# Early gated attention of a fused kernel: scans of four pairs, masks, key copies and products of two, scores in quarters of the array

## The chip, the cores and the metric

The kernel runs on one core of a Trainium2 chip. The metric is the time of one launch on the device in microseconds, and lower is better. TensorE (PE) multiplies matrices, VectorE (DVE), ScalarE (ACT) and GpSimd (POOL) do the elementwise work, and SyncE (SP) issues most of the DMAs. The first section of the kernel uses all of them at once.

## The reference

What is computed is a gated linear attention and, on its output, two expert layers in turn (4 x 768 = 3072 tokens, 8 heads of 48, width 384).

```python
for t in range(S):
    state = alpha[:, :, t, :, None] * state + np.einsum('bhd,bhe->bhde', k[:, :, t], v[:, :, t])
    y[:, :, t] = np.einsum('bhd,bhde->bhe', q[:, :, t], state)
...
h = x @ w_in                       # 384 -> 2048
x = (h * sigmoid(h)) @ w_out       # 2048 -> 384
g = x @ w_gate                     # 384 -> 1536
return (silu(g) * (x @ w_val)) @ w_out2
```

All tensors are float32 in value; the weights come as 64-bit floats and are decoded to 32 bits on the chip.

## The kernel before, in words

The sequence of each batch is cut into chunks of C = 128 tokens: 6 x 4 = 24 chunks, each with 8 heads in NP = 4 pairs. A pair lies on the 128 partitions, head 0 on rows 0 to 47 and head 1 on rows 64 to 111. Per pair the decay from each token to the end of its chunk is a product of alphas, made by a scan that runs backward (`stage_a1`, tile `r`); its counterpart from the start, scaled by the reciprocal of the whole, is made by a second scan (`stage_a3`, tile `g`). Keys are multiplied by `r`, queries by `g` (tile `kq`). Then the scores of a head are one product, a causal mask makes `pt` of them, and the output `y` (in the accumulator `yd`) is `pt` times values plus the queries times the carried state. The state of the next chunk needs the keys transposed (`kt`, made by a product with the identity) times the values.

The first NF = 7 chunks, 28 pairs, are made ahead of everything else; this document calls them the early attention. In it the products run in full float32. A "duo" d is two pairs, so a chunk is duos 2n and 2n + 1. The scans, the reciprocals and the products with keys and with queries are issued per duo, the masks, key copies and score products per pair. The loop `for g in range(first): attn(2)` writes the instructions in the order in which each engine runs them; nothing reorders them afterwards. `filler` puts a bfloat16 product without use ahead of scores, into accumulator columns that are overwritten later. `spread` (GpSimd) lays out the values of pair 0 of the first four chunks once more, so that its rows can be added into the other pairs' spare rows. `chunk_high` and `chunk_end` split the finished output into a high and a low part (`x`), add up the state, and load the values of chunk n + 2 (`load_v`). The input of chunk n + 2 (`load_in`) is loaded into one of two buffers once chunk n's products have been made.

Beside this, `units1` decodes weights of the first expert layer. One unit is 128 x 384 weights: three steps on VectorE (`decode`, L93, L98 and L103), then a high part on ScalarE and a low part on GpSimd or VectorE. In the early attention one call of `units1` follows each chunk from the third on, with the three steps belonging to two neighbouring units.

After the early attention the expert layer begins: `g1(0)` is the hidden product of the first block (tokens of chunks 0 to 3), `act1` its activation in two parts, `gh` (ScalarE) and `gl` (VectorE, L322), and `g2` the second product, which needs `gh` at L770 and L771 and `gl` at L773. The other 17 chunks of attention (the late attention) are made beside the expert layer, with their scores in high and low parts (`qh`, `ql`, `kh`, `kl`).

Of the kernel before, what the change touches and what calls it, by code (L numbers as in the profile page):

```python
# [20 lines left out]
DM = H * D  # L21
# [247 lines left out]
def fast(ctx, tc, pk, w1, w2, out, bad_i):  # L269
# [49 lines left out]
    cp.tile([128, 112], F32, name="edge")  # L319
# [12 lines left out]
    qh = ac.tile([128, NP, 2 * C + 2 * D], F32R, name="qh")  # L332
    ql = ac.tile([128, NP, 2 * C], F32R, name="ql")
    kts = [ac.tile([128, 2, 64], F32, name=f"kt{i}") for i in range(NP + 1)]
# [3 lines left out]
    ones = ac.tile([128, 2, CA], F32, name="ones")  # L338
    rc_t = [ac.tile([128, 2, CA], F32, name=f"rc{i}") for i in range(2)]
# [5 lines left out]
    p0 = [start[:, (7 + 2 * i) * C:(9 + 2 * i) * C].rearrange("p (h t) -> p h t", h=2) for i in range(2)]  # L345
# [52 lines left out]
    def KF(d):  # L398
        return DVE if d == 0 else POOL

    def stage_a1(d):
        n, ps_, _ = duo(d)
        lo = ps_.start * CA
        r = r_t[d] = ap.tile([128, 272], F32, tag="r", name=f"r{d}")[:, :2 * CA].rearrange(
# [5 lines left out]
            data1=ones.rearrange("p i t -> p (i t)")[:, ::-1], initial=0.0,  # L412
# [3 lines left out]
    def stage_a2(d):  # L416
        n, ps_, _ = duo(d)
        kq_t[d] = ap.tile([128, 2, 2, C], F32, tag="kq", name=f"kq{d}", bufs=6)
        DVE.reciprocal(out=rc_t[d % 2][:, :, 0], in_=r_t[d][:, :, 0])  # L419
        KF(d).tensor_tensor(  # L420
            out=kq_t[d][:, 0], in0=in_t[n][1][:, 0, ps_], in1=r_t[d][:, :, 1:], op=ALU.mult
        )

    def stage_a3(d):
        n, ps_, (c, b) = duo(d)
        lo = ps_.start * CA
        gg = ap.tile([128, 272], F32, tag="g", name=f"g{d}")[:, :2 * CA].rearrange(
# [4 lines left out]
            data1=rc_t[d % 2].rearrange("p i t -> p (i t)"), initial=0.0,  # L432
            op0=ALU.mult, op1=ALU.add,
        )
        (DVE if d == 0 else POOL).tensor_tensor(
# [3 lines left out]
        if c and n < NF:  # L439
            for i in range(ps_.start, ps_.stop):  # L440
                s = state[b][:, i]
                ACT.activation(out=s, in_=s, func=AF.Copy, scale=r[:, i - ps_.start, 0:1])
        elif c:
# [10 lines left out]
    def q_parts(d):  # L454
        _, ps_, _ = duo(d)
        for h in range(2):
            r, cs = slice(64 * h, 64 * h + 64), slice(C * h, C * h + C)
            yield qh[r, ps_, cs], ql[r, ps_, cs], kq_t[d][r, 1], h

    def stage_b(d):  # L460
        kh = kh_t[d] = ap.tile([128, 2, C], F32R, tag="kh", name=f"kh{d}")
# [4 lines left out]
    def stage_c(d):  # L466
        kl = kl_t[d] = ap.tile([128, 2, C], F32R, tag="kl", name=f"kl{d}")
# [4 lines left out]
    def guard(d):  # L472
# [3 lines left out]
            out=jk, in_=kq_t[d].rearrange("p x i t -> p (x i t)"), func=AF.Square,  # L476
            accum_out=sums[:, ps_.start // 2, n:n + 1],
# [5 lines left out]
    def qkt(g):  # L483
# [3 lines left out]
        kf, qf = kq_t[d][:, 0, i], kq_t[d][:, 1, i]  # L487
        if n < NF:

            b = pools_ps["early"].tile([128, 2, 512], F32, tag=f"s{g % 2}", name=f"s{g}")  # L490
            for h in range(2):
                r = slice(64 * h, 64 * h + 64)
                PE.matmul(b[:, h, :C], kf[r], qf[r], start=True, stop=True)
            PE.matmul(b[:, 0, C:C + 2 * D], kf, columns(ident), start=True, stop=True)
            s_t[g] = b[:, :, :C], b[:, 0, C:C + 2 * D]
            return
        b = bank(5, f"s{g}")
        w = 2 * C + (2 * D if n < NCH - B else 0)
        kh, kl = kh_t[d][:, i], kl_t[d][:, i]
        PE.matmul(b[:, :w], kh, qh[:, p, :w], start=True, stop=False)  # L500
# [9 lines left out]
    def filler(g):  # L510


        n, i = divmod(g, NP)


        if n and i < 2:
            return
        if n not in y_t:
            yd_place(n)
        wide = mask.rearrange("p (o t) -> p o t", o=1).to_broadcast([128, 4, C])  # L520
        for _ in range(3 if 0 < g < NP + 2 else 1):
# [3 lines left out]

    def causal(g):
        if g < NE * NP and g % NP == 0:
# [1053 lines left out]
```

## Time and profile before

| | before |
|---|---|
| time, median of 3 runs | 936.69 us (935.79 to 937.24) |
| the profiled execution | 938.12 us, of which the span is 936.3 us |
| TensorE | 915.2 us busy, 98% of the span |
| VectorE, ScalarE, GpSimd | 618.1, 453.0, 287.9 us busy |
| granted TensorE clock | 0.992 on average |
| HBM | 118 MB read, 30 MB written |

The span is the time from the first to the last instruction of the profiled execution; its 938.12 us include what lies around it. Busy shares are averages over a program that has stages with different limits, so the rows below are taken from single stages.

### The profile page before, as it was taken

The numbers are of one execution on the slowest core, as the hardware profiler recorded it, in microseconds if no ns is written. First come the engines' busy times: TensorE is split into PE (matmuls) and PEld (weight loads), VectorE is DVE, ScalarE is ACT, GpSimd is POOL, SyncE is SP. The second block draws the span as 40 slices with busy tenths as digits, with TensorE's granted clock in tenths as the row PEclk, the third lists the DMA queues.
The fourth block names the chain that finished last, engine by engine and source line by source line (L and its number), as shares of the span: only waits on it lengthen the run. The fifth ranks groups of instructions, "written<-read, shape, count | busy, mean of one in ns | idle before, by whom it ended". The sixth has DMA issues, their size and how long they took to land.

```text
span 936.3 us, 14380 instructions
## 1 busy us (share of the span) xinstructions
PE 915.2 (98%) x5210; PEld 779.6 (83%) x5210; DVE 618.1 (66%) x1107; ACT 453.0 (48%) x1019; POOL 287.9 (31%) x401
## 2 busy tenths in 40 slices
PE   9989999999999999999999999999999999999996
PEld 5669998889999998988888888878888888888785
DVE  8889936656577668465268366786477875577732
ACT  3545435646465565555346344543544454444432
POOL 5430006528779789686228000000000000000000
PEclk9899999999999999999999999999999999999998
DMA  7854203243645554532375486532757503755302
GB/s 235 300 187 153 85 1 105 80 142 119 194 160 194 167 175 161 181 108 101 118 264 208 157 299 224 185 114 85 244 213 267 194 10 135 269 205 214 121 0 71
DMA packets 43007, 150.89 MB, mean 161 GB/s; under 512 B 4400, under 2 KB 9008, under 8 KB 40240
## 3 DMA queue, kind: packets, MB, share of 16 engines
q1 hardware_dynamic: 42304, 149.30, 46.3%
q8 instruction: 43, 0.70, 0.3%
q10 hardware_dynamic: 624, 0.59, 0.2%
q14 instruction: 36, 0.29, 0.1%
HBM read 118.03 MB, written 29.88 MB: 158 GB/s over the span
## 4 chain that ended last, share of the span: by engine, by line
PE 89%; DVE 5%; issue 2%; DMA 1%; POOL 1%; ACT 1%; SPq 0%; ACTq 0%; POOLq 0%; DVEq 0%
PE o L1158 15%; PE h L721 7%; PE x L773 7%; PE x L770 7%; PE x L771 7%; PE h L722 7%; PE h L724 7%; PE A L1095 5%; PE D L1095 5%; PE E L1095 5%; PE yd L562 2%; PE K L1095 2%; PE F L1095 2%; PE C L1095 2%; PE B L1095 2%; PE G L1095 2%
## 5 line engine op out<-in xcount | busy, mean ns | idle before, releaser
L322 DVE TENSOR_TENSOR gl<-h,gh 128x384 fp32r<-128x384 f32 (+1 forms) x112 | 68.5, 612 | 89.8 <-ACT h L739 84.4
L721 PE MATMUL h<-x,w 128*128 128x384 f32 (+1 forms) x336 | 122.7, 365 | 1.8 <-DMA x<-y 1.8
L770 PE MATMUL x<-gh,w 128*128 128x384 f32 (+1 forms) x336 | 121.5, 362 | 0.4 <-ACT gh L738 0.4
L771 PE MATMUL x<-gh,w 128*128 128x384 f32 (+1 forms) x336 | 121.2, 361 | 0.0
L722 PE MATMUL h<-x,w 128*128 128x384 f32 (+1 forms) x336 | 120.9, 360 | 0.0
L738 ACT ACTIVATE gh<-h 128x384 fp32r<-128x384 f32 (+1 forms) x112 | 59.9, 534 | 105.3 <-PE h L724 103.4
L1158 PE MATMUL o<-gh,ring 128*128 128x512 f32 x288 | 88.8, 389 | 0.0
L773 PE MATMUL x<-gl,w 128*128 128x384 f32 (+1 forms) x336 | 84.5, 359 | 1.6 <-DVE gl L322 1.6
L724 PE MATMUL h<-x,w 128*128 128x384 f32 (+1 forms) x336 | 84.3, 358 | 0.0
L420 POOL TENSOR_TENSOR kq<-in,r 128x256 f32<-128x256 f32 x47 | 43.0, 915 | 130.1 <-DVE rc L419 76.3
L721 PEld LDWEIGHTS h<-x,w 128*128 128x128 f32 x336 | 63.1, 188 | 10.6 <-issue 5.4
L770 PEld LDWEIGHTS x<-gh,w 128*128 128x128 f32 x336 | 63.1, 188 | 6.7 <-ACT gh L738 1.1
L773 PEld LDWEIGHTS x<-gl,w 128*128 128x128 f32 x336 | 61.3, 188 | 8.1 <-DVE gl L322 2.3
L771 PEld LDWEIGHTS x<-gh,w 128*128 128x128 f32 x336 | 63.1, 188 | 5.2
L722 PEld LDWEIGHTS h<-x,w 128*128 128x128 f32 x336 | 63.1, 188 | 5.1
L724 PEld LDWEIGHTS h<-x,w 128*128 128x128 f32 x336 | 61.3, 188 | 5.9
L1158 PEld LDWEIGHTS o<-gh,ring 128*128 128x128 f32 x288 | 54.1, 188 | 11.2
L739 ACT ACTIVATE h<-h 128x384 f32<-128x384 f32 (+1 forms) x112 | 59.5, 532 | 0.0
L322 DVE TENSOR_TENSOR gl<-a,gh 128x512 fp32r<-128x512 f32 x48 | 32.9, 692 | 37.3 <-ACT gh L1147 36.2
L1158 PE MATMUL o<-gl,ring 128*128 128x512 f32 x144 | 56.4, 392 | 0.8 <-DVE gl L322 0.8
L1095 PE MATMUL A<-mov,ring 128*128 128x512 f32 x198 | 55.7, 389 | 0.0
L1095 PE MATMUL D<-mov,ring 128*128 128x512 f32 x198 | 55.6, 389 | 0.0
(211 smaller groups left out, 1983.3 us busy)
## 6 DMA issues: line engine op xcount, KB each, us to landing
ring<-comb_d SPq DMA_DIRECT2D x21, 1920.0 KB, 7.7
raw<-in_w_dram SPq DMA_DIRECT2D x58, 384.0 KB, 4.4
in<-in_pk_dram SPq DMA_DIRECT2D x22, 770.5 KB, 4.4
ring<-wo_d SPq DMA_DIRECT2D x6, 1920.0 KB, 7.3
comb_d<-area SPq DMA_DIRECT2D x8, 896.0 KB, 5.4
in_v<-in_pk_dram SPq DMA_DIRECT2D x24, 256.0 KB, 3.7
comb_d<-area SPq DMA_DIRECT2D x8, 640.0 KB, 4.9
x1r<-x_d SPq DMA_DIRECT2D x6, 768.0 KB, 8.9
```

What stands on the lines that cost most here:

```text
L322: eng.tensor_tensor(out=lo, in0=src, in1=hi.bitcast(F32), op=ALU.subtract)
L420: KF(d).tensor_tensor(out=kq_t[d][:, 0], in0=in_t[n][1][:, 0, ps_], in1=r_t[d][:, :, 1:], op=ALU.mult)
L721: PE.matmul(acc, part(u, k), xh, start=(k == 0), stop=False)
L722: PE.matmul(acc, part(u, k, 1), xh, start=False, stop=False)
L724: PE.matmul(acc, part(u, k), xl, start=False, stop=(k == len(xk) - 1))
L738: ACT.activation(out=gh, in_=hb, func=AF.Silu)
L739: ACT.activation(out=hb, in_=hb, func=AF.Silu)
L770: PE.matmul(x1_t[j][m], part(u, m), gh, start=(f == 0), stop=False)
L771: PE.matmul(x1_t[j][m], part(u, m, 1), gh, start=False, stop=False)
L773: PE.matmul(x1_t[j][m], part(u, m), gl, start=False, stop=(f == NF1 - 1))
L1095: PE.matmul(acc, s(hs, r), x[:, hx], start=op in new and i == 0, stop=i == 2, skip_group_check=True,)
L1158: PE.matmul(o_t[b][m], part(ring_t[p, f], m, l), x, start=(f == 0 and i == 0), stop=(f == NF2 - 1 and i == 2),)
```

## The change

The early attention gets functions of its own, and the loop over pairs becomes a loop over duos (`early`).

- Scans: `scan_r` and `scan_g` run over all four pairs of a chunk (516 elements instead of 258), with one reciprocal of four elements. Chunk 0 alone keeps two halves.
- Products: keys and queries of a duo lie side by side and are multiplied in one instruction of 512 elements (GpSimd; VectorE for the first duo). A duo's tile has 48 more columns that hold parts of the identity, written once at the start into six fixed tiles (`kqs`).
- Scores: a head's product with the queries and its product with the identity become one, whose moving operand is 176 columns wide. It is issued for half of the keys at a time, so that it takes 64 rows and 64 columns of the array: 8 products for a duo (`scores2`).
- Mask and key copy: one instruction for a duo instead of one for a pair (`mask2`, `keys2`).
- Decode: from chunk 3 on `early_unit` runs all three steps of one unit in a row; its temporary lies in columns of the accumulator `yd` of the next chunk, which are not yet in use, and no longer in SBUF.
- The tiles of the late attention (`qh`, `ql` and others) are opened, zeroed (GpSimd) and filled with the identity (ScalarE, four copies) between the early attention and `g1(0)` instead of at the start (`open_late`).
- Fillers: one for each duo, four ahead of the second duo.

On VectorE this stands for one chunk and a little more before (names are tiles: `r`, `g` the scans, `pt` and `start` the masks, `x` the low part of an output, `dec` and `raw` a decode):

```order
L409 SCALAR_TENSOR_TENSOR r_422<-in_332,ones 128x258
L419 RECIPROCAL rc_115<-r_422 128x2
L430 SCALAR_TENSOR_TENSOR g_452<-in_332,rc_115 128x258
L93 TENSOR_SCALAR dec_0_457<-raw_0_189 128x384
L532 TENSOR_TENSOR pt_459<-s_448,mask 128x256
L532 TENSOR_TENSOR pt_471<-s_467,mask 128x256
L409 SCALAR_TENSOR_TENSOR r_475<-in_332,ones 128x258
L419 RECIPROCAL rc_116<-r_475 128x2
L322 TENSOR_TENSOR x_309<-yd_381,x_309 128x3x128
L532 TENSOR_TENSOR pt_490<-s_486,mask 128x256
L430 SCALAR_TENSOR_TENSOR g_493<-in_332,rc_116 128x258
L532 TENSOR_TENSOR pt_506<-s_502,mask 128x256
```

and here for the same part after (`rg` the scans, `rc` the reciprocals, `yd` and `raw` the decode in the accumulator):

```order
L422 SCALAR_TENSOR_TENSOR rg_115<-in_270,ones_113 128x516
L427 RECIPROCAL rc_114<-rg_115 128x4
L474 TENSOR_TENSOR pt_397<-s_368,mask 128x512
L435 SCALAR_TENSOR_TENSOR rg_115<-in_270,rc_114 128x516
L93 TENSOR_SCALAR yd_366<-raw_0_178 128x384
L98 SCALAR_TENSOR_TENSOR yd_366<-raw_0_178,yd_366 128x384
L103 SCALAR_TENSOR_TENSOR raw_0_178<-raw_0_178,yd_366 128x384
L322 TENSOR_TENSOR x_273<-yd_300,x_273 128x3x128
L474 TENSOR_TENSOR pt_431<-s_422,mask 128x512
```

Four scans of 258 have become two of 516, four masks two. The scan of the next chunk's queries, the whole decode and the subtraction now follow each other, and the mask of the chunk's second duo stands behind them.

On TensorE these are, before, the scores of the last three pairs of chunk 3 and the first of chunk 4, behind which the value products of chunk 3 stand (`s` the scores, `yd<-mask` the filler):

```order
L493 MATMUL s_448<-kq_344 128x128 x2
L494 MATMUL s_448<-start,kq_344 128x96
L522 LDWEIGHTS mask
L522 MATMUL yd_465<-mask 128x512
L493 MATMUL s_467<-kq_393 128x128 x2
L494 MATMUL s_467<-start,kq_393 128x96
L522 LDWEIGHTS mask
L522 MATMUL yd_465<-mask 128x512
L493 MATMUL s_486<-kq_393 128x128 x2
L494 MATMUL s_486<-start,kq_393 128x96
L493 MATMUL s_502<-kq_424 128x128 x2
L494 MATMUL s_502<-start,kq_424 128x96
```

and after, with chunk 3's second duo, chunk 4's first, and the first value products of chunk 3:

```order
L609 LDWEIGHTS mask
L609 MATMUL yd_366<-mask 128x512
L463 MATMUL s_422<-kq_118 64x176 x8
L609 LDWEIGHTS mask
L609 MATMUL yd_439<-mask 128x512
L463 MATMUL s_441<-kq_119 64x176 x8
L650 MATMUL yd_366<-pt_397,in_v_343 64x128
```

The scores of a pair were two products of 64 rows and one of 128; a duo's are now eight of 64 rows and 64 columns. The value products of a chunk now follow the scores of the next chunk's first duo instead of its first pair.

On SP's queue, from the load of chunk 2's input on, before (`in` inputs, `in_v` values, `raw` weights):

```order
L365 DMA in_187<-in_pk_dram 128x1541
L689 DMA raw_0_189<-in_w_dram 128x768
L689 DMA raw_1_191<-in_w_dram 128x768
L365 DMA in_253<-in_pk_dram 128x1541
L689 DMA raw_2_298<-in_w_dram 128x768
L389 DMA in_v_318<-in_pk_dram 128x512
L365 DMA in_332<-in_pk_dram 128x1541
L689 DMA raw_3_334<-in_w_dram 128x768
```

and after:

```order
L385 DMA in_190<-in_pk_dram 128x1541
L385 DMA in_211<-in_pk_dram 128x1541
L385 DMA in_270<-in_pk_dram 128x1541
L409 DMA in_v_277<-in_pk_dram 128x512
L787 DMA raw_2_280<-in_w_dram 128x768
L787 DMA raw_3_298<-in_w_dram 128x768
L385 DMA in_337<-in_pk_dram 128x1541
L409 DMA in_v_343<-in_pk_dram 128x512
```

The load of the values of chunk n + 2 stood ahead of the load of the input of chunk n + 4; now it stands behind it.

```diff
-    def KF(d):
-        return DVE if d == 0 else POOL
+    def scan_r(n, i, k):
+        rg, cs = rg4[n % 2], slice(i * CA, (i + k) * CA)
+        DVE.tensor_tensor_scan(
+            out=rg[:, 0, cs][:, ::-1], data0=in_t[n][0][:, cs.start + 1:cs.stop + 1][:, ::-1],
+            data1=ones4[:, i:i + k].rearrange("p i t -> p (i t)")[:, ::-1], initial=0.0,
+            op0=ALU.mult, op1=ALU.add,
+        )
+        DVE.reciprocal(
+            out=rc4[:, i:i + k, 0], in_=rg[:, 0].rearrange("p (i t) -> p i t", i=NP)[:, i:i + k, 0]
+        )
+    def scan_g(n, i, k):
+        rg, cs = rg4[n % 2], slice(i * CA, (i + k) * CA)
+        DVE.tensor_tensor_scan(
+            out=rg[:, 1, cs], data0=in_t[n][0][:, cs],
+            data1=rc4[:, i:i + k].rearrange("p i t -> p (i t)"), initial=0.0, op0=ALU.mult, op1=ALU.add,
+        )
+        by_pair = rg.rearrange("p x (i t) -> p x i t", i=NP)
+        for lo in range(i, i + k, 2):
+            d = (n * NP + lo) // 2
+            kq_t[d] = kqs[d % 6]
+            (DVE if d == 0 else POOL).tensor_tensor(
+                out=kq_t[d][:, :, :2 * C].rearrange("p i (x t) -> p x i t", x=2),
+                in0=in_t[n][1][:, :, lo:lo + 2], in1=by_pair[:, :, lo:lo + 2, 1:], op=ALU.mult,
+            )
+        c, b = divmod(n, B)
+        if c:
+            for p in range(i, i + k):
+                t = state[b][:, p]
+                ACT.activation(out=t, in_=t, func=AF.Copy, scale=by_pair[:, 0, p, 0:1])
+        if i + k == NP:
+            load_in(n + 2)
+    def scores2(d):
+        b = pools_ps["early"].tile([128, 2, 512], F32, tag=f"s{d % 2}", name=f"s{d}")
+        for i in range(2):
+            for h in range(2):
+                r, cs = slice(64 * h, 64 * h + 64), slice(i * (C + D), (i + 1) * (C + D))
+                for t in (slice(0, 64), slice(64, 128)):
+                    PE.matmul(
+                        b[t, h, cs], kq_t[d][r, i, t], kq_t[d][r, i, C:], start=True, stop=True,
+                        skip_group_check=True,
+                    )
+        return b[:, :, :2 * (C + D)].rearrange("p h (i x) -> p i h x", i=2)
+    def mask2(d, s):
+        pt = ap.tile([128, 2, 2, C], F32, tag="pt", name=f"pt{d}", bufs=3)
+        pt_t[2 * d], pt_t[2 * d + 1] = pt[:, 0], pt[:, 1]
+        wide = mask.rearrange("p (a o t) -> p a o t", a=1, o=1).to_broadcast([128, 2, 2, C])
+        DVE.tensor_tensor(out=pt, in0=s[:, :, :, :C], in1=wide, op=ALU.mult)
+    def keys2(d, s):
+        t = kts[d % 3]
+        kt_t[2 * d], kt_t[2 * d + 1] = (t[:, i].rearrange("p h x -> p (h x)") for i in range(2))
+        ACT.activation(out=t[:, :, :, :D], in_=s[:, :, :, C:], func=AF.Copy)
+    def early(d):
+        m, odd = divmod(d, 2)
+        if m not in y_t:
+            yd_place(m)
+        filler(m, 4 if d == 1 else 1)
+        s = scores2(d)
+        if not odd and m:
+            pv(m - 1)
+        mask2(d, s)
+        keys2(d, s)
+        if odd:
+            if m and m + 2 < NF:
+                scan_r(m + 2, 0, NP)
+        elif m + 1 < NF:
+            if m < 2:
+                scan_r(m + 1, 0, NP)
+            scan_g(m + 1, 0, NP)
+        if m < NE and odd == (m == 0):
+            spread(m)
+        if not odd and m:
+            if m >= 3:
+                early_unit(yd_t[m][:, 512:])
+            chunk_high(m - 1)
+            chunk_end(m - 1)
+        up_to("gd", d - 1, guard, ND)
+        up_to("l1", d, load1, NU1)
...
-        kf, qf = kq_t[d][:, 0, i], kq_t[d][:, 1, i]
-        if n < NF:
-            b = pools_ps["early"].tile([128, 2, 512], F32, tag=f"s{g % 2}", name=f"s{g}")
-            for h in range(2):
-                r = slice(64 * h, 64 * h + 64)
-                PE.matmul(b[:, h, :C], kf[r], qf[r], start=True, stop=True)
-            PE.matmul(b[:, 0, C:C + 2 * D], kf, columns(ident), start=True, stop=True)
-            s_t[g] = b[:, :, :C], b[:, 0, C:C + 2 * D]
...
-    def filler(g):
...
+    def filler(n, times):
         wide = mask.rearrange("p (o t) -> p o t", o=1).to_broadcast([128, 4, C])
-        for _ in range(3 if 0 < g < NP + 2 else 1):
+        for _ in range(times):
             PE.matmul(
                 yd_t[n][:, :512].rearrange("p (o t) -> p o t", o=4), mask, wide, start=True, stop=True
             )
...
+    def decode_in(key, bank_):
+        if raw_t[key].dtype != F32:
+            dec_t[key] = bank_.bitcast(I32)[:, :DM]
+            in_bank.add(key)
+        for i in range(3):
+            decode_unit(key, i)
...
+    def early_unit(bank_):
+        u = st["d1"]
+        up_to("s1", st["h1"] - 1, lambda u: low_unit(("1", u), POOL), NU1)
+        up_to("h1", st["f1"] - 1, lambda u: high_unit(("1", u), wp, "w"), NU1)
+        if u < st["l1"]:
+            decode_in(("1", u), bank_)
+            for k in "d1", "e1", "f1":
+                st[k] = u + 1
...
     make_identity(nc, ident)
+    for t in kqs:
+        one, two = (
+            ident[:, c:c + D].rearrange("p (o d) -> p o d", o=1).to_broadcast([128, 2, D]) for c in (0, 64)
+        )
+        POOL.tensor_tensor(out=t[:, :, 2 * C:], in0=one, in1=two, op=ALU.add)
...
-    POOL.memset(qh.bitcast(F32), 0.0)
-    POOL.memset(ql.bitcast(F32), 0.0)
...
     first = NF * NP
-    st["b"] = st["c"] = first // 2
-    stage_a(0)
-    stage_a(1)
     up_to("l1", 1, load1, NU1)
-    for i in range(NP):
-        ACT.activation(
-            out=qh[:, i, 2 * C:].rearrange("p (h d) -> p h d", h=2), in_=columns(ident), func=AF.Copy
-        )
-    T0 = 2
-    for g in range(first):
-        attn(2)
-        if g % 2:
-            up_to("l1", g // 2, load1, NU1)
+    for i in (0, 2):
+        scan_r(0, i, 2)
+        scan_g(0, i, 2)
+    for d in range(first // 2):
+        early(d)
+    st["qk"], st["pv"] = first, NF - 1
+    for k in "a1", "a2", "a3", "b", "c":
+        st[k] = first // 2
...
     need1(1)
     units1()
     attn(1, False)
+    up_to("gd", first_d - 1, guard, ND)
+    estack.close()
+    open_late()
     g1(0)
     rest = act1(*steps[0])
     units1()
```

## Rows read from the trace of the kernel before

**Rows 1.** Stages of the span; busy us (instructions) by engine, granted clock, DMA share.

```profile
0.00:58.10 58.10, 52.41 (x506) 36.26 (x506) 49.26 (x102) 26.35 (x96) 28.18 (x51) 0.91 0.73 255
67.00:120.00 53.00, 52.98 (x275) 48.72 (x274) 52.14 (x115) 26.26 (x56) 0.51 (x1) 1.00 0.38 129
```

**Rows 2.** Groups of instructions in the stage 0 to 58.1 us.

```profile
L430 DVE TENSOR_TENSOR_SCAN g<-in,rc 128x258 f32<-128x258 f32 x14 | 12.2, 869 | 1.0 <-DVE rc L419 0.5
L409 DVE TENSOR_TENSOR_SCAN r<-in,ones 128x258 f32<-128x258 f32 x14 | 11.8, 845 | 2.0 <-DMA in<-in_pk_dram 1.9
L532 DVE TENSOR_TENSOR pt<-s,mask 128x256 f32<-128x256 f32 x24 | 9.6, 412 | 2.6 <-PE s L494 2.6
L419 DVE RECIPROCAL rc<-r 128x2 f32<-128x2 f32 x14 | 2.4, 168 | 0.5
L435 POOL TENSOR_TENSOR kq<-in,g 128x256 f32<-128x256 f32 x13 | 9.3, 718 | 10.3 <-DVE g L430 10.3
L593 POOL COPY start<-in_v 128x96 f32<-128x96 f32 x4 | 1.8, 462 | 0.0
L612 ACT ACTIVATE x<-yd 128x384 fp32r<-128x384 f32 x6 | 2.9, 485 | 0.0
L1350 ACT ACTIVATE qh<-start 128x96 fp32r<-128x96 f32 x4 | 0.8, 270 | 0.6 <-POOL qh L1337 0.6
```

**Rows 3.** Order of time, from the last mask to the first low part.

```profile
55.72 0.41 DVE L532 TENSOR_TENSOR pt<-s,mask 128x256 f32<-128x256 f32 x1
58.13 0.50 PE L721 MATMUL h<-x,w 128*128 128x512 f32 x1
60.57 0.49 ACT L644 ACTIVATE x<-yd 48x384 fp32r<-48x384 f32 x1 [1.93 <-DVE y L322]
66.19 0.97 PE L773 MATMUL x<-gl,w 128*128 128x512 f32 x3 [1.60 <-DVE gl L322]
```

**Rows 4.** Order of time, a scan alone and one beside GpSimd.

```profile
6.12 0.69 DVE L409 TENSOR_TENSOR_SCAN r<-in,ones 128x258 f32<-128x258 f32 x1
6.90 0.68 POOL L420 TENSOR_TENSOR kq<-in,r 128x256 f32<-128x256 f32 x1 [1.37 <-DVE r L409]
7.05 1.08 DVE L430 TENSOR_TENSOR_SCAN g<-in,rc 128x258 f32<-128x258 f32 x1
```

**Rows 5.** Groups of decoding before 55.8 us; one such step through PSUM later.

```profile
L93 DVE TENSOR_SCALAR dec<-raw 128x384 int32<-128x384 int32 x4 | 2.8, 707 | 0.1
L103 DVE SCALAR_TENSOR_TENSOR raw<-raw 128x384 int32<-128x384 int32 x3 | 2.5, 821 | 0.0
L98 DVE SCALAR_TENSOR_TENSOR raw<-raw,dec 128x384 int32<-128x384 int32 x3 | 2.0, 668 | 0.0
...
473.03 0.56 DVE L98 SCALAR_TENSOR_TENSOR dec<-raw,dec 128x384 int32<-128x384 int32 x1
```

**Rows 6.** Order of time on TensorE, score blocks, value and state products.

```profile
24.36 0.49 PE L493 MATMUL s<-kq 64*128 64x128 f32 x4
25.18 0.45 PE L562 MATMUL yd<-pt,in_v 128*64 128x128 f32 x4
27.15 0.38 PE L493 MATMUL s<-kq 64*128 64x128 f32 x2
...
49.51 0.65 PE L583 MATMUL yd<-kq,state 64*48 64x128 f32 x16
```

**Rows 7.** DMA issues of 0 to 60 us: the values of a chunk.

```profile
in_v<-in_pk_dram SPq DMA_DIRECT2D x8, 256.0 KB, 5.7
```

**Rows 8.** Seconds of the stage, columns as in group 1.

```profile
35.00:36.00 1.00, 0.24 (x2) 0.00 (x0) 0.96 (x3) 0.00 (x0) 0.57 (x1) 1.00 1.03 419
37.00:38.00 1.00, 1.00 (x6) 0.78 (x6) 0.97 (x3) 0.68 (x3) 0.33 (x1) 0.50 0.99 386
43.00:44.00 1.00, 1.00 (x16) 0.54 (x8) 1.00 (x2) 0.00 (x0) 0.32 (x1) 0.63 1.01 388
65.00:66.00 1.00, 0.00 (x0) 0.00 (x0) 1.00 (x2) 0.42 (x1) 0.12 (x1) 1.00 0.51 174
```

More of the change, by code (lines that the diff above doesn't have):

```diff
@@ L331, in fast @@
     ac = astack.enter_context(tc.tile_pool(name="ac", bufs=1))
-    qh = ac.tile([128, NP, 2 * C + 2 * D], F32R, name="qh")
-    ql = ac.tile([128, NP, 2 * C], F32R, name="ql")
-    kts = [ac.tile([128, 2, 64], F32, name=f"kt{i}") for i in range(NP + 1)]
+    kts = [ac.tile([128, 2, 2, 64], F32, name=f"kt{i}") for i in range(3)]
     jk = ac.tile([128, 4 * C], BF16, name="jk")
@@ L337, in fast, with open_late @@
     mask = ac.tile([128, C], BF16, name="mask")
-    ones = ac.tile([128, 2, CA], F32, name="ones")
-    rc_t = [ac.tile([128, 2, CA], F32, name=f"rc{i}") for i in range(2)]
+    estack, lstack = ExitStack(), ExitStack()
+    ep = estack.enter_context(tc.tile_pool(name="ep", bufs=1))
+    ones4 = ep.tile([128, NP, CA], F32, name="ones4")
+    rc4 = ep.tile([128, NP, CA], F32, name="rc4")
+    rg4 = [ep.tile([128, 2, NP * CA], F32, name=f"rg{i}") for i in range(2)]
+    kqs = [ep.tile([128, 2, 2 * C + D], F32, name=f"kq{i}") for i in range(6)]
+    late_t = {}
+    def open_late():
+        lp = late_t["pool"] = lstack.enter_context(tc.tile_pool(name="lp", bufs=2))
+        for name, w, dtype in (("qh", 2 * C + 2 * D, F32R), ("ql", 2 * C, F32R)):
+            late_t[name] = lp.tile([128, NP, w], dtype, tag=name, name=name, bufs=1)
+            POOL.memset(late_t[name].bitcast(F32), 0.0)
+        for i in range(NP):
+            ACT.activation(
+                out=late_t["qh"][:, i, 2 * C:].rearrange("p (h d) -> p h d", h=2), in_=columns(ident),
+                func=AF.Copy,
+            )
+        for name in ("ones", "rc0", "rc1"):
+            t = late_t[name] = lp.tile([128, 2, CA], F32, tag=name, name=name, bufs=1)
+            POOL.memset(t, 0.0)
+        POOL.memset(late_t["ones"][:, :, C:], 1.0)
     start = big(0, "start")
@@ L411, in stage_a1 @@
             data0=in_t[n][0][:, lo + 1:lo + 2 * CA + 1][:, ::-1],
[L412 removed]
+            data1=late_t["ones"].rearrange("p i t -> p (i t)")[:, ::-1], initial=0.0,
             op0=ALU.mult, op1=ALU.add,
@@ L438, in stage_a3 @@
         r = r_t.pop(d)
[L439 to L443, printed above, removed]
+        if c:
             POOL.tensor_tensor(
@@ L475, in guard @@
         ACT.activation(
-            out=jk, in_=kq_t[d].rearrange("p x i t -> p (x i t)"), func=AF.Square,
-            accum_out=sums[:, ps_.start // 2, n:n + 1],
+            out=jk.rearrange("p (x t) -> p x t", x=2),
+            in_=kq_t[d][:, :, :2 * C] if n < NF else kq_t[d].rearrange("p x i t -> p x (i t)"),
+            func=AF.Square, accum_out=sums[:, ps_.start // 2, n:n + 1],
         )
@@ L584, in pv @@
                     y[r:r + D, p * C:p * C + C], state[b][hs, p],
-                    kq_t[(first + p) // 2][hs, 1, p % 2], start=False, stop=True,
+                    kq_t[(first + p) // 2][(hs, p % 2, slice(C, 2 * C)) if n < NF else (hs, 1, p % 2)],
+                    start=False, stop=True,
                     skip_group_check=True,
@@ L695, in decode_unit @@
                 dec_t[key] = mp.tile([128, DM], I32, tag="dec", name="dec%s_%d" % key, bufs=1)
-            x = decode(DVE, raw_t[key], dec_t[key], step, inplace=key[0] == "2" and key[1] >= NW)
+            x = decode(DVE, raw_t[key], dec_t[key], step, inplace=key in in_bank)
             if step == 2:
@@ L956, in units_o @@
         if f < NF2:
-            if raw_t["2", NW + f].dtype != F32:
-                dec_t["2", NW + f] = bank(5, f"dec{f}").bitcast(I32)[:, :DM]
-            for i in range(3):
-                decode_unit(("2", NW + f), i)
+            decode_in(("2", NW + f), bank(5, f"dec{f}"))
     FIRST = (
@@ L1237, in attn @@
             new = st["qk"]
-            if new < NF * NP:
-                filler(new)
             qkt(new)
@@ L1319, in fast @@
     DVE.memset(jk, 0.0)
-    for t in [ones] + rc_t:
+    for t in (ones4, rc4):
         DVE.memset(t, 0.0)
-    DVE.memset(ones[:, :, C:], 1.0)
+    DVE.memset(ones4[:, :, C:], 1.0)
     DVE.memset(warm, 0.0)
```

79 lines of the change are left out of this document (27 added, 52 removed).

## The prediction

> **What bounds the kernel now.** I read the table of stages first, then the groups of instructions in the first stage, then the order of time around the places that change. The table of stages [rows 1] shows what the average hides: from 67 us on TensorE is busy without a gap, so nothing in the first attention can gain there except by letting it begin sooner. Before that come 58.1 us in which VectorE is busy 49.3 us and TensorE 52.4, and neither all the time. Who decides is seen in the groups: VectorE's two kinds of scan take 12.2 and 11.8 us, 24 of its 28 masks 9.6 us, and its whole idle time ahead of these is 2.6 us, for scores of TensorE [rows 2]. GpSimd's products, 0.72 us each, are short against that. So the first 58 us are a chain through VectorE, with GpSimd and TensorE taking turns behind it. What counts is T, the moment at which the first hidden product of the expert layer starts (58.13 us), and the moment at which TensorE gets the low part it then waits for (66.19 us) [rows 3]. Everything later I take to move along with that second moment, because the work after it is the same and TensorE has no gap there.
>
> **The sum's footing.** The profiled execution took 938.1 us (span 936.3), 1.4 us over the median 936.7 of the runs shown. I add to 938.1 and take 1.4 off at the end.
>
> **Scans.** 28 scans of 258 elements become 4 of 258 (chunk 0) and 12 of 516. A scan with GpSimd idle takes 0.69 us; the one that runs beside a GpSimd product takes 1.08 [rows 4]. So of the 24.0 us now, 28 x 0.69 = 19.3 are the scans and 4.7 are overlap with GpSimd. No row shows 516 elements. It is at most 2 x 0.69 = 1.38, and at least that less one instruction's fixed part, for which a two-element reciprocal of 0.17 is the nearest row [rows 2]: 1.21. I take 1.3, nearer the upper end since the fixed part is surely under that of a reciprocal. That gives 4 x 0.69 + 12 x 1.3 = 18.4. Behind the second scan of a chunk now stand operations that read PSUM while GpSimd multiplies, and the masks among the rows, which read PSUM, stay at 0.41; so I keep 2.0 of the 4.7 us of overlap. The scans then cost 20.4, a gain of 3.6 us; the ends are 0 (1.38 each, all the overlap) and 6.7 (1.21, none).
>
> **Reciprocals and masks.** Six reciprocals go: 6 x 0.17 = 1.0 us. 28 masks of 0.41 (11.5 us) become 14 of twice the width, between 0.65 and 0.82 by the same reasoning; at 0.73 that is 10.2, a gain of 1.3 us (0 to 2.4).
>
> **Decode by way of PSUM.** Up to the last mask of the early stage VectorE now spends 2.8 + 2.5 + 2.0 = 7.3 us on decoding, three units and a first step, much of it stretched by GpSimd [rows 5]. After the change four whole units stand there. The same steps through PSUM are in the trace later, at 0.56 us each [rows 5], so about 1.7 us a unit: 6.8 us, a gain of 0.5 (between -1.5, if they stretch like the old ones to 2.2 us a unit, and 0.5).
>
> So VectorE loses 3.6 + 1.0 + 1.3 + 0.5 = 6.4 us of work on the way to T. The idle 2.6 us before masks mostly go too, since there are half as many of them and the scores come in one piece: 2.0 (0 to 2.6).
>
> **Scores in quarters.** One pair's scores and key product take TensorE 0.82 us, from 24.36 to the next products at 25.18 [rows 6]. For two pairs there are now 8 products, 16 instructions of 176 columns on quarters of the array. The trace has quarters: the 16 state products of 128 columns take 0.65 us in all [rows 6], so 0.65 x 176/128 = 0.9 us for two pairs instead of 1.64. Were they as slow as the two heads of now, whose four instructions of 128 columns take 0.49 us to their end, it would be up to 0.49 x 4 x 176/128 = 2.7. I take 0.9: it is the same form. TensorE's work falls by 14 x 0.74 = 10 us, but that lies beside VectorE, so it enters only through waits.
>
> **New waits.** One product for two pairs, keys and queries, is 1.4 us on GpSimd (two of 0.70, at most two of 0.9 by my estimate from the stretched scans) where the first pair's keys could start after 0.7. Four places follow from the order of VectorE shown with the change.
> First, chunk 1: after its second scan VectorE has one mask (0.73), while product (1.4), hand-overs (0.3) and scores (0.9) must pass: 1.9 us of waiting.
> Second, the first output of chunk 0: its products need the spread values, and that copy (0.46) stands on GpSimd behind three products (4.2). With 2.0 us of products (25.18 to 27.15 [rows 6]), 0.7 us of ScalarE [rows 2] and 0.2 of hand-overs the subtraction can start 7.6 us after the scan, where VectorE's own work and the first wait reach it at about 6.3: 1.3 us.
> Third, the same for chunk 1, where VectorE is later: 0.4 us.
> Fourth, at chunk 5 no scan stands ahead of the subtraction any more: 0.7 us.
> Together 4.3 us (1.5 to 8). From chunk 3 on, decoding (1.7), a mask, and two scans (2.6) stand between the mask that releases the value products and the subtraction that reads them, 5 us against 2.7, so nothing is late there. That also covers the value load, which now stands behind the next input on SP's queue; it takes 5.7 us to land [rows 7], and 2.3 us of lateness would be free.
>
> **The clock.** By the same durations the scores and fillers of chunk 0 end near 10.4 us, and chunk 1's first product, behind a second scan that ends near 12.0, near 13.4: a pause of 3 us on TensorE. In this trace the granted clock fell from 1.00 to 0.50 (2.4 to 1.2 GHz) after the second 35 to 36 us, in which TensorE was busy 24%, and was back in the course of the second 43 to 44 us, after work without a gap [rows 8]. So I expect the lower level for one stretch early on: the 2.0 us of value products of chunk 0 and a score block double, about 2 us on TensorE, 1.0 of it on the chain.
>
> **T and the hand-over.** T = 58.1 - 6.4 - 2.0 + 4.3 + 1.0 = 55.0 us, the tail from the last mask to T (55.72 to 58.13 [rows 3]) kept. Behind T something goes too: now VectorE is deep in decoding, so that ScalarE waits 1.93 us for its subtraction and starts on the block's rows at 60.57 [rows 3]; afterwards one decode step stands ahead, and I count 1.5 of the 1.93 us as gained. Against this, ScalarE gets four copies (0.8 us in all now, at the start [rows 2]) ahead of the first activation, and GpSimd the memsets before them, beside VectorE's decoding. ScalarE idled for part of that stretch, so I count half the copies, 0.4 us. Net, the low part arrives at T + 6.96 instead of T + 8.06, so 62.0 against 66.19: a gain of 4.2 us. 938.1 - 4.2 = 933.9, and by the runs' median 932.5 us.
>
> **The rivals.**
> Forecast: VectorE's shorter work less the new waits, 932.5 us; its own range is 929.5 to 934.8, 3.0 us less of waits and scans to 2.3 us more. Chance 0.50.
> The whole saving shows: GpSimd's overlap with the scans all but gone (gain 6.7 instead of 3.6), the clock never falls (1.0 less). Then 4.2 + 3.1 + 1.0 = 8.3 us, 928.4 us. For it speaks that GpSimd's products now fall into operations on PSUM; against it the 3 us pause. Chance 0.17.
> The saving is eaten: waits at their upper end (8.0 instead of 4.3), because the pairs of products run at 0.9 us a half and the values come late. Then the gain is 4.2 - 3.7 = 0.5 us, 936.2 us. What speaks for it: GpSimd has half as many starts, and each is twice as long to wait for. Chance 0.16.
> Slower: TensorE, with less work, falls to 1.2 GHz and stays there through chunks 1 to 6, and becomes the bound. A chunk at full clock is two score blocks (1.8), value products (2.0 to 2.3) and two fillers (0.6), 4.5 us, against 6.9 on VectorE (masks 1.5, scans 2.8, decode 1.7, subtraction and gaps 0.9); at half clock it is 9.0, so 2.1 us more per chunk. Gain and loss cross at two such chunks; with four the time is 936.7 - 4.2 + 8.4 = 940.9 us. For it speaks the idle third of each chunk; against it that a TensorE which is the bound works without a gap, and behind such work the clock came back at 43 to 44 us [rows 8]. Chance 0.17.
> The Trainium skill (TensorE: Matmul & The Clock Gate, Part 1) has this rule in a sharper form: "the default state is throttled, and activity releases the throttle". By that rule the pauses of each chunk would throttle it anew and the slower case would be the likely one; the trace agrees in the fall between 35 and 38 us, but shows the full clock too in 65 to 66 us, in which TensorE did nothing [rows 8].
>
> **How the numbers follow.** A difference of 0.2% (1.9 us) is about what can be told from none. The forecast and the whole saving lie beyond it on the fast side: 0.67. The eaten saving is within it: 0.16. The slower case: 0.17. The range runs from 927.5, just under the whole saving, to 939.0, into the slower case at three chunks, which leaves about a tenth out at either end.
>
> **What would show it.** In the profile after: scans of 516 elements at 1.2 to 1.4 us and their sum near 20; masks near 0.73; a score block of 16 instructions near 0.9 us (a block over 1.6 would refute the quarters); VectorE waiting for scores of chunk 1 and for ScalarE at the first output; the clock at 0.50 for one early stretch; T near 55 and the first wait for the low part ending near 62. Wrong I would be above all if the clock stays low (T over 60), if the new waits are as long as the work saved, or if TensorE gets gaps behind 67 us that it does not have now.

## The result, and the profile after

| | before | after |
|---|---|---|
| time, median | 936.39 us (4 runs) | 949.13 us (948.57 to 949.81, 4 runs) |
| the profiled execution's span | 936.3 us | 948.0 us |
| granted TensorE clock | 0.992 | 0.989 |

The kernel became slower: ratio 1.0136, interval 1.0118 to 1.0153. The forecast was 932.5 us. The table of stages of after, in the columns of [rows 1], begins with the stretch that T ends; the four next lines are stretches in which the clock fell, the last is a second much later:

```profile
0.00:55.65 55.65, 42.00 (x557) 27.71 (x557) 40.41 (x67) 23.72 (x78) 25.69 (x40) 0.88 0.78 259
10.00:15.00 5.00, 2.33 (x27) 1.45 (x25) 2.69 (x5) 0.94 (x3) 2.52 (x3) 0.72 0.75 308
15.00:20.00 5.00, 4.84 (x56) 3.81 (x52) 3.66 (x6) 1.51 (x5) 2.05 (x2) 0.60 0.45 161
28.00:31.00 3.00, 2.82 (x39) 2.70 (x39) 1.64 (x4) 0.06 (x2) 2.45 (x3) 0.71 0.95 260
45.00:50.00 5.00, 4.64 (x52) 3.00 (x53) 3.02 (x7) 2.65 (x9) 2.85 (x3) 0.66 0.76 254
190.00:191.00 1.00, 1.00 (x5) 1.00 (x4) 0.00 (x0) 0.00 (x0) 0.00 (x0) 0.50 0.20 76
```

In the first stage VectorE is busy 40.4 us instead of 49.3, TensorE 42.0 instead of 52.4, and T has moved from 58.13 to 55.68 us [rows 3]. The early attention did get shorter. The groups of that stage answer to [rows 2]:

```profile
L435 DVE TENSOR_TENSOR_SCAN rg<-in,rc 128x516 f32<-128x516 f32 (+1 forms) x8 | 8.9, 1110 | 0.1
L422 DVE TENSOR_TENSOR_SCAN rg<-in,ones 128x516 f32<-128x516 f32 (+1 forms) x8 | 9.4, 1174 | 1.7 <-DMA in<-in_pk_dram 1.7
L474 DVE TENSOR_TENSOR pt<-s,mask 128x512 f32<-128x512 f32 x14 | 9.5, 678 | 5.6 <-PE s L463 5.6
L427 DVE RECIPROCAL rc<-rg 128x4 f32<-128x4 f32 (+1 forms) x8 | 1.4, 178 | 0.3
L443 POOL TENSOR_TENSOR kq<-in,rg 128x512 f32<-128x512 f32 x13 | 16.0, 1253 | 18.4 <-DVE rg L435 8.6 <-ACT state L451 6.4 <-ACT x L701 3.2
L98 DVE SCALAR_TENSOR_TENSOR yd<-raw,yd 128x384 int32<-128x384 int32 x4 | 2.3, 563 | 0.1
L609 PE MATMUL yd<-mask 128*128 128x512 bf16 x17 | 6.7, 422 | 5.0 <-DVE raw L103 3.9 <-ACT state L762 0.7 <-ACT jk L578 0.3
```

The scans take 8.9 + 9.4 = 18.3 us instead of 24.0, the 14 masks 0.68 us each. The order of time answers to [rows 3, 6]: two score blocks, then the last mask, T, and the hand-over behind it.

```profile
13.04 1.45 PE L463 MATMUL s<-kq 64*64 64x176 f32 x16 [2.67 <-POOL kq L443]
20.09 0.83 PE L463 MATMUL s<-kq 64*64 64x176 f32 x16
...
53.32 0.68 DVE L474 TENSOR_TENSOR pt<-s,mask 128x512 f32<-128x512 f32 x1
55.68 0.50 PE L819 MATMUL h<-x,w 128*128 128x512 f32 x1
59.03 1.28 POOL L351 MEMSET qh<- 128x1408 f32 x1 [7.87 <-ACT jk L578]
60.34 0.80 ACT L353 ACTIVATE qh<-start 128x96 fp32r<-128x96 f32 x4 [1.37 <-POOL qh L351]
61.17 0.60 ACT L836 ACTIVATE gh<-h 128x512 fp32r<-128x512 f32 x1
61.82 0.50 PE L868 MATMUL x<-gh,w 128*128 128x512 f32 x1 [1.69 <-ACT gh L836]
63.32 0.85 PE L871 MATMUL x<-gl,w 128*128 128x512 f32 x3
```

The first product that needs the low part starts at 63.32 us, against 66.19 before [rows 3]. So at that moment the kernel after is 2.9 us ahead, and the expected gain was 4.2. The 12.7 us of loss must come later, in the part where, by the prediction, nothing changes.

I laid the product groups of the two traces beside each other, in order. After is ahead by 2.8 us at 103 us and by 2.2 at 178. At 206, behind the stretch at the lower clock (last line of the first table), it is ahead by only 0.55, and stays at 0.4 to 0.6 until 325 us, where the blocks of 384 columns run. From about 400 us on, where the products have 512 columns again, it falls behind steadily. These are places of that stretch on TensorE, before:

```profile
522.22 0.84 PE L1095 MATMUL A<-mov,first 128*128 128x512 f32 x3
...
700.22 0.84 PE L1095 MATMUL E<-mov,ring 128*128 128x512 f32 x3
700.89 0.84 PE L1095 MATMUL A<-mov,ring 128*128 128x512 f32 x3
...
925.70 2.20 PE L1158 MATMUL o<-ahl,ring 128*128 128x512 f32 x9
```

and the same places after:

```profile
523.67 0.86 PE L1190 MATMUL A<-mov,first 128*128 128x512 f32 x3
...
705.93 0.87 PE L1190 MATMUL E<-mov,ring 128*128 128x512 f32 x3
706.64 0.85 PE L1190 MATMUL A<-mov,ring 128*128 128x512 f32 x3
...
937.33 2.26 PE L1253 MATMUL o<-ahl,ring 128*128 128x512 f32 x9
```

From the first to the last of them it takes 925.70 - 522.22 = 403.5 us before and 937.33 - 523.67 = 413.7 after, 2.5% longer, with hardly a wait in either. The groups in the middle show it in the small: a group of three products takes 0.67 us to the next one before, and 0.71 after. Over four such groups (700.22 to 702.93 and 705.93 to 708.72 us) a product takes 2.71/12 = 0.226 and 2.79/12 = 0.2325 us, 2.9% more. The same in the groups of 600 to 900 us (busy us, mean ns of one, idle), before:

```profile
L1158 PE MATMUL o<-gh,ring 128*128 128x512 f32 x237 | 73.1, 389 | 0.0
L1095 PE MATMUL E<-mov,ring 128*128 128x512 f32 x159 | 44.7, 389 | 0.0
```

and after:

```profile
L1253 PE MATMUL o<-gh,ring 128*128 128x512 f32 x216 | 67.8, 395 | 0.0
L1190 PE MATMUL E<-mov,ring 128*128 128x512 f32 x162 | 46.4, 394 | 0.0
```

389 against 395 ns, at a granted clock of 1.00 in both. At 0.233 us a product there are some 2,100 in the 489 us from 427 to 916 us; 6 ns more for each makes 12.6 us. The offset between the traces grew by 12.0 us in that stretch. So the loss is a slower product of 512 columns, and none of the instructions that the change rewrote.

What in the change could reach these products is a line of the diff which the section on the change leaves out and the prediction did not price:

```diff
-    cp.tile([128, 112], F32, name="edge")
+    cp.tile([128, 80], F32, name="edge")
```

`edge` is never read or written. It only takes up room at the left end of SBUF, so the tiles allocated behind it from that side lie 32 x 4 = 128 bytes lower (a few of them 1,664, which is 128 beyond a multiple of 512): the moving operands of the late products (`mov`, `gh`, `gl`, `x`, `y3`) go from multiples of 512 bytes (the first `mov` at 67,072) to 128 bytes under one (66,944). The weights (`w`, `ring`) are allocated from the right end, behind `edge_r`, and stay at multiples of 512 (130,560).

### The profile page after: what moved, and what is told of

It reads as the page before. It is cut to its first block, busy times and chain, and to the rows that moved or that the text cites. A ratio compares the mean times of both kernels' runs of the same rounds, so it can differ in the third digit from the quotient of the medians.

```text
span 948.0 us, 14403 instructions
## 1 busy us (share of the span) xinstructions
PE 919.7 (97%) x5261; PEld 773.3 (82%) x5261; DVE 609.6 (64%) x1073; ACT 451.4 (48%) x1005; POOL 287.2 (30%) x396
## 4 chain that ended last, share of the span: by engine, by line
PE 87%; DVE 7%; issue 2%; ACT 1%; DMA 1%; POOL 0%; SPq 0%; ACTq 0%; POOLq 0%; DVEq 0%
PE o L1253 16%; PE h L819 6%; PE x L868 6%; PE x L869 6%; PE x L871 6%; PE h L822 6%; PE h L820 6%; PE A L1190 5%; PE D L1190 5%; PE E L1190 5%; PE yd L650 2%; PE K L1190 2%; PE B L1190 2%; PE G L1190 2%; PE F L1190 2%
## 5 line engine op out<-in xcount | busy, mean ns | idle before, releaser
L527 POOL TENSOR_TENSOR kq<-in,r 128x256 f32<-128x256 f32 x34 | 33.9, 998 | 116.2 <-DVE r L516 116.2
```

The source lines that it names most:

```text
L527: POOL.tensor_tensor(out=kq_t[d][:, 0], in0=in_t[n][1][:, 0, ps_], in1=r_t[d][:, :, 1:], op=ALU.mult)
```

## The experiments

**Where the tiles lie, or the change's code?** Theory A: the addresses make the products slow. Theory B: the changed code does. Two kernels are the kernel before with nothing but addresses moved, two are the kernel after with its moving tiles at multiples of 256 bytes again.

`b_edge80` is before with the left tile of after, `b_right` before with the weights moved instead:

```diff
-    cp.tile([128, 112], F32, name="edge")
+    cp.tile([128, 80], F32, name="edge")        # b_edge80
-    edge.tile([128, 120], F32, name="edge_r")
+    edge.tile([128, 88], F32, name="edge_r")    # b_right
```

Expected of `b_edge80`: 

> The kernel before with nothing changed but one unused filler tile in SBUF: 80 columns instead of 112, so that all tiles of the left side, the moving operands of the expert layers among them, lie 128 bytes lower, as they do in the changed kernel. Theory A (products of 512 columns run slower because of where their operands lie): TensorE's step of 512 columns goes from 0.2267 to about 0.233 us behind 430 us, and the time to about 949 (936.4 + some 12 to 13). Theory B (the slower step comes from the change's own code): 936.4 us, step 0.2267.

Expected of `b_right`: 

> The kernel before with the filler tile of the right side at 88 columns instead of 120: the weights (w, ring) lie 128 bytes higher, the moving operands stay. If it is the moving operand's address that counts: 936.4 us. If the stationary operand's address, or the difference between the two, counts: 945 to 950 us. Theory B: 936.4 us.

Measured: `b_edge80` 950.61 us, ratio 1.0157 (1.0124 to 1.0190); `b_right` 951.70 us, ratio 1.0157 (1.0127 to 1.0187). The groups of 600 to 900 us, of `b_edge80` and then of `b_right`:

```profile
L1095 PE MATMUL E<-mov,ring 128*128 128x512 f32 x165 | 47.3, 395 | 0.0
```

```profile
L1095 PE MATMUL E<-mov,ring 128*128 128x512 f32 x165 | 47.3, 395 | 0.0
```

395 ns in both, with the instructions of before. One line that changes no instruction makes the whole loss, and it does not matter which of the two operands is moved.

The blocks of 384 columns are slower too, by less. Their products with `gl` in 206 to 325 us, of before and then of `b_edge80`:

```profile
L773 PE MATMUL x<-gl,w 128*128 128x384 f32 x90 | 20.4, 334 | 0.0
```

```profile
L773 PE MATMUL x<-gl,w 128*128 128x384 f32 x91 | 21.0, 338 | 0.0
```

From one to the next it is 173 ns in before and 175 in `b_edge80`, `b_right` and after, and `b_edge80` falls behind before by 0.5 us across these 119 us. In after that is hidden: `a_edge48` below, which has its code without the slower products, gets 0.4 us further ahead of before in the same stretch.

`a_align` is after with `edge` back at 112; the room comes from one tile for three small ones, with one memset in place of three, and a shorter pad. `a_edge48` is after with `edge` at 48, which puts the moving operands at 256 above a multiple of 512:

```diff
-    cp.tile([128, 80], F32, name="edge")
+    cp.tile([128, 112], F32, name="edge")       # a_align
-        for name in ("ones", "rc0", "rc1"):
-            t = late_t[name] = lp.tile([128, 2, CA], F32, ...)
+        three = lp.tile([128, 3, 2, CA], F32, tag="three", name="three", bufs=1)
...
+    cp.tile([128, 48], F32, name="edge")        # a_edge48
```

Expected of `a_align`: 

> The changed kernel with the filler tile at 112 columns again; room for it is made by three small tiles sharing one and by 8 unused columns less in each input tile. Theory A: step 0.2267 us, and what the early stage gained is seen: 932.5 to 935 us (2.9 us ahead at the first low part in the changed kernel's trace, less up to 1.5 for a stretch at half clock near 190 us). Theory B: 949 us, step 0.233.

Expected of `a_edge48`: 

> The changed kernel with the filler tile at 48 columns, so that the left tiles lie at 256 beyond a multiple of 512 bytes. Theory A in the form 'a multiple of 256 is enough': 933 to 935 us. Theory A in the form 'a multiple of 512': 949 us. Theory B: 949 us.

Measured: `a_align` 936.58 us (933.23 to 939.41), ratio 0.9985 (0.9964 to 1.0006); `a_edge48` 934.70 us (933.68 to 936.81), ratio 0.9975 (0.9959 to 0.9992). The groups of 600 to 900 us, of `a_align` and then of `a_edge48`:

```profile
L1191 PE MATMUL E<-mov,ring 128*128 128x512 f32 x159 | 44.7, 389 | 0.0
```

```profile
L1190 PE MATMUL E<-mov,ring 128*128 128x512 f32 x157 | 44.2, 389 | 0.0
```

389 ns in both, with the products of after. Theory A holds from both sides and B falls. A distance of 256 bytes costs nothing. `a_align` missed its range for the time (932.5 to 935) by 1.6 us. Its trace has two stretches of about 3 us at a granted clock of 0.50, at 189 and 356 us; each costs 1.5 us against before.

**Each operand by itself, or one against the other?** `b_both` moves both ends by the same 128 bytes:

```diff
-    edge.tile([128, 120], F32, name="edge_r")
+    edge.tile([128, 152], F32, name="edge_r")
-    cp.tile([128, 112], F32, name="edge")
+    cp.tile([128, 80], F32, name="edge")
```

> The kernel before with both unused edge tiles changed (left 112 to 80 columns, right 120 to 152), so that the moving operands and the weights all lie 128 bytes lower: each off a multiple of 256 bytes, but not off each other. Theory R (what counts is where the two operands lie to each other): as before, 936.9 us, a ratio of 1.000, and 0.2267 us for a 512-column product. Rival M (each operand must lie at a multiple of 256 bytes by itself): 950 us or more, ratio 1.0157 or above, since either shift alone cost that much; 0.2333 us for a product, or more if both count.

Measured: 937.61 us, ratio 1.0007 (0.9990 to 1.0023).

```profile
L1095 PE MATMUL E<-mov,ring 128*128 128x512 f32 x159 | 44.6, 389 | 0.0
```

389 ns: theory R holds. Neither operand needs a multiple of 256 bytes; they only have to lie alike. Each of these edits moves everything on its side of SBUF. That the moving tile and the weight tile are the two that count is read from the products that got slower; no run moves one tile alone.

**How far off?** `b_edge104` and `b_edge96` are before with `edge` at 104 and 96 columns, 32 and 64 bytes off.

Expected of `b_edge104`: 

> The kernel before with the left edge tile at 104 instead of 112 columns: the moving operands lie 32 bytes off the weights' multiple of 256. Theory P (either they lie alike within 256 bytes or they do not): 0.2333 us per 512-column product and 950.6 us, as with 128 bytes. Rival G (the cost grows with the distance): a quarter of 14 us, 940.4.

Expected of `b_edge96`: 

> The kernel before with the left edge tile at 96 columns: 64 bytes off. Theory P: 950.6 us. Rival G: half of 14 us, 943.9. A third reading (what counts is a multiple of 64 bytes): 936.9 here and 950.6 with 32 bytes; but 128 bytes cost the full amount, which speaks against it.

Measured, in two runs each: 951.05 us, ratio 1.0144 (1.0126 to 1.0162), and 950.05 us, ratio 1.0133 (1.0116 to 1.0151). The group of `b_edge104`; that of `b_edge96` has the same numbers:

```profile
L1095 PE MATMUL E<-mov,ring 128*128 128x512 f32 x162 | 46.6, 396 | 0.0
```

396 ns already at 32 bytes. Theory P holds and G falls: the cost does not grow with the distance.

**What is left of the early gain, and where could it be more?** With the tiles in place, two parts of the new early stage came out otherwise than predicted: fillers that wait for a decode, and a wait at the hand-over. `a48_nofill` leaves out those fillers, `a48_late` opens the late tiles later, `a48_two` does both; all have `edge` at 48.

```diff
-        filler(m, 4 if d == 1 else 1)
+        if not (odd and m >= 3):                 # a48_nofill
+            filler(m, 4 if d == 1 else 1)
...
-    open_late()
     g1(0)
     rest = act1(*steps[0])
     units1()
     rest()
+    open_late()                                  # a48_late
```

Expected of `a48_nofill`: 

> The changed kernel with the left edge tile at 48 columns (934.7 us, 0.9975 of before), and without the filler product of a chunk's second two pairs from chunk 3 on, which waits for the decoding of a weight unit (4 products of 512 columns are left out, nothing else). Theory D: these products held up the scores and so VectorE's masks; the 5.3 us of TensorE's waits at the filler go, VectorE's 4.9 us of waits for scores fall to about 2.5, the first expert product starts 2 us earlier (52.3 instead of 54.3 us), and the time is 932.7, ratio 0.9954. Rival: the next wait (GpSimd's products, the state) takes its place or the clock falls without the filler, and the first expert product stays within 0.5 us of 54.3; ratio 0.9975.

Measured: 933.84 us, ratio 0.9954 (0.9936 to 0.9971), as theory D said; but the first expert product starts at 53.75 us, 0.57 earlier than in `a_edge48`, which is the rival's size. Its waits (us in total, times, longest):

```profile
PE yd L610 <- ACT state L763: 4.2, 4, 1.6
DVE pt L474 <- PE s L463: 3.2, 2, 1.7
PE yd L610 <- ACT jk L579: 3.0, 1, 3.0
```

The wait for the decode is gone, that of the masks fell only to 3.2, and the fillers that are left wait for ScalarE's state and guard instead. So D is wrong in its size: the time agrees with it, but the trace gives a quarter of the 2 us, and the intervals of this ratio and of that of `a_edge48` overlap. Nor does the 0.57 us stand by itself, since the second profile of `a_edge48` has this product at 55.31 us, 0.99 later than the first. What speaks for an effect is that the two kernels without these fillers are the earliest (53.75 us, and 53.99 in `a48_two` below), and the six profiles with them have 54.21 to 55.68. That is about 1 us, with its size left open.

Expected of `a48_late`: 

> The changed kernel with the left edge tile at 48 columns, and the opening of the late attention's tiles (five memsets on GpSimd, four copies on ScalarE) moved behind the first expert activation. Theory H: TensorE's wait for the first activation (1.8 us) falls to 0.5 or less, since the copies no longer stand ahead of it on ScalarE; the second moment comes 1.4 us earlier and the time is 933.3, ratio 0.996. Rival: the low part behind it (VectorE, and the block's rows on ScalarE) is late anyway, so the wait moves there and the time stays at 934.7, ratio 0.9975.

Measured: 933.83 us, ratio 0.9960 (0.9946 to 0.9973). The first expert product, the first that needs the activation and the first that needs the low part, in `a_edge48`:

```profile
54.32 0.50 PE L819 MATMUL h<-x,w 128*128 128x512 f32 x1
60.46 0.50 PE L868 MATMUL x<-gh,w 128*128 128x512 f32 x1 [1.77 <-ACT gh L836]
62.16 1.48 PE L871 MATMUL x<-gl,w 128*128 128x512 f32 x3
```

and in `a48_late`:

```profile
54.21 0.50 PE L819 MATMUL h<-x,w 128*128 128x512 f32 x1
58.45 0.39 PE L868 MATMUL x<-gh,w 128*128 128x512 f32 x1
60.19 0.98 PE L871 MATMUL x<-gl,w 128*128 128x512 f32 x3 [0.22 <-DVE gl L322]
```

From the first to the third it takes 7.84 us there and 5.98 here; the wait of 1.77 us is gone, 0.22 is left at the low part. Theory H holds for the trace.

Expected of `a48_two`: 

> Both edits of the two kernels before this one together (no filler of the second two pairs from chunk 3 on, 4 products left out; the late tiles opened behind the first activation). If both theories hold and add up: 2.0 + 1.4 us less than 934.7, so 931.3 us, ratio 0.994. If the first fails: 933.3. If both fail: 934.7, 0.9975.

Measured: 932.43 us (930.01 to 934.76), ratio 0.9940 (0.9914 to 0.9966). The median lies between 931.3 and 933.3 and the interval holds all three cases, so this run does not tell them apart. In its trace the gains do not add up: the low part comes 6.86 us behind the first expert product, against 5.98 in `a48_late`.

Two of these were timed again, side by side. Expected of `a_edge48_b`: 

> The changed kernel with the left edge tile at 48 columns, a second time, now beside the version that opens the late tiles later: ratio to before 0.9975, 934.7 us. If its first time was by chance below before, the ratio is 1.000.

Expected of `a48_late_b`: 

> The same with the late attention's tiles opened behind the first activation, a second time. If the 1.4 us of the first activation's wait is kept to the end: 1.4 us below the kernel beside it, 933.3, ratio 0.996. If it is given back later: the same time as that one within 0.4 us.

Measured: 934.59 us, ratio 0.9968 (0.9956 to 0.9981), and 934.07 us, ratio 0.9966 (0.9948 to 0.9985). `a_edge48` is faster than before twice over. Between the two the medians differ by 0.5 us with runs 6 us apart: whether the 1.4 us of the hand-over reach the end is not shown by the times. In the traces of this pair the late one is 1.5 us ahead at the low part (61.49 against 62.96 us) and 1.4 us at the last product group.

## Why the prediction was wrong

**The step that failed** is "Everything later I take to move along with that second moment, because the work after it is the same and TensorE has no gap there". The work is the same and there is no gap, but the price of each instruction is not: 512-column products went from 0.226 to 0.2325 us because the change moved one of their operands by 128 bytes, some 12 us from 427 us on. The premise that TensorE has no gap was read too far as well: [rows 1] shows 67 to 120 us, and at 190 us before waits 1.6 us for a block's rows. The sum had no term for where tiles lie. None of the rivals had it either; the slower one (TensorE at half clock through the early chunks) did not occur, T being 55.68 and not over 60. The prediction's own signal for being wrong, gaps behind 67 us, did not appear: a TensorE that is 100% busy can still be slower.

**With the tiles in place** the kernel takes 934.7 and 934.6 us, 2.2 and 2.7 under before timed beside them, where the forecast had 4.2 under. The traces say the same. The second moment lies at 64.76 to 66.19 us in the six profiles with the code of before (mean 65.4) and at 62.16 to 63.32 in the four with the early stage and the hand-over of after (mean 62.7). That is 2.6 us on average, where the one comparison above has 2.9. The part on the early stage is therefore right in sign and too large by some 1.5 to 2 us. Term by term, from the trace of after:

- VectorE's work to T: 49.26 - 40.41 = 8.9 us less [rows 1], predicted 6.4. Scans 18.3 us (predicted 20.4: 516 elements take less than the 1.3 us taken, and hardly stretch), masks 14 x 0.68 = 9.5 (10.2), reciprocals 1.4 (1.4), decoding 4 x 1.66 = 6.6 (6.8; its middle step has 0.56 us, as in [rows 5]).
- VectorE's idle time to T: 55.65 - 40.41 = 15.2 us against 58.10 - 49.26 = 8.8 before, 6.4 more. Predicted were 3.3 (4.3 of new waits and 1.0 of clock less 2.0). This is the term that was under-sized. The 2.6 us that the prediction calls the "whole idle time" is that ahead of the masks alone; the two rows of scans in [rows 2] have 3.0 us more. The waits of 0 to 75 us after:

```profile
DVE pt L474 <- PE s L463: 5.6, 5, 2.2
PE yd L609 <- DVE raw L103: 3.9, 2, 2.4
DVE x L322 <- ACT x L701: 3.8, 3, 1.9
```

- Of the four places where waits were priced, chunk 1's first scores came out at 2.2 us (1.9 predicted; the longest of the first line), the first output at 0.9 (1.3, with 0.7 us of ScalarE in it where the row that it cites has 0.485), chunk 1's at nothing (0.4), chunk 5's at 1.0 (0.7). Not priced was chunk 2's output, 1.9 us, the longest of the third line: GpSimd's copy of the spread values stood behind two products there, and TensorE waited 1.9 us for it at 28.18 us.
- The second line holds what was overlooked. The reasoning for chunk 3 and later ("so nothing is late there") looked at the value products, but not at the filler: that of a chunk's second duo writes the accumulator tile in which the decode of the same chunk has its temporary, and waits for the decode's last step, up to 2.4 us, with the scores behind it. In `a48_nofill` the wait is gone and other waits took most of its place; about 1 us at T is left of it.
- Score block 0.83 us (predicted 0.9), the quarters as expected; 1.45 at the lower clock.
- Product of a duo: 1.25 us on GpSimd (1.4 taken, 1.8 at most).
- Clock: the pause ended at 13.04 us (predicted 13.4), and the level fell to 0.50 (1.2 GHz) around it. But the rows show three stretches with the lower level in them, 10 to 20, 28 to 31 and 45 to 50 us (means 0.60 to 0.72), and one was priced.
- T: 55.68, predicted 55.0; 54.32 and 55.31 in the two profiles of `a_edge48`. That the sum came out right is luck: too small a saving (6.4 for 8.9) stood against too small a wait (3.3 for 6.4).
- Hand-over: 7.64 us behind T, predicted 6.96, before 8.06. The four copies and the memsets ahead of the first activation were taken at 0.4 us. GpSimd's memset waits for ScalarE's guard, ScalarE's copies for the memset, the activation stands behind the copies. `a48_late` puts their price at 7.84 - 5.98 = 1.9 us; the second pair of profiles has 1.7.

The Trainium skill (TensorE: Matmul & The Clock Gate, Part 1) was quoted for throttling anew after each pause. The early stage shows three stretches at 0.50, nearer to that rule than the one I counted; TensorE did not stay there.

**Open.** In after the clock is at 0.50 for about 3 us from 190 us on (last line of the first table above), behind a wait of 1.7 us for a block's rows, and its lead over before falls from 2.15 to 0.55 us across it. Before has a wait of 1.6 us at the same place and keeps its clock at 1.00 there. Of the two profiles of the kernel that opens the late tiles later, one keeps 1.00 in that place and the other falls to 0.50, so the code alone does not decide it. But six of the eight profiles with the code of after fall there, and none of the six with the code of before. A second such place is at about 356 us, where three of each kind fall. Each fall costs about 1.5 us. No run was made to tell why.

## What to carry to other kernels

A diff has to be read for the addresses that it moves too: a pad, an unused tile or a changed pool size shifts everything allocated behind it, and a product far from the change can get dearer with no wait in the profile. Compare the step from one product to the next of the same shape in both traces before looking for waits. And where a stage on the way to a bound engine gets shorter, count what stands queued at the hand-over with its dependencies, not with its durations.

## What the runs showed of the hardware

- A 512-column product took 389 ns in the trace (0.226 us from one to the next) where the moving tile and the weight tile lay at the same address modulo 256 bytes (distances of 0 and 256), and 395 to 396 ns (0.2325 us) where they lay 32, 64 or 128 bytes off each other. Over these distances it is a step and no slope, and only the difference of the two counts (both moved by 128 bytes: 389 ns). What in the chip makes it is not shown.
- Products of 384 columns lose less: 173 ns from one to the next against 175, 334 against 338 ns in the trace (before and `b_edge80`, 206 to 325 us).
- A scan of 516 elements took 1.22 to 1.25 us in ten of twelve cases, under twice the 0.69 of 258 [rows 4], also where GpSimd multiplied beside it (1.23 at 24.77 us). The first one, with 1.85 us, and one with 1.35, both beside work of GpSimd, are the exceptions.
